# A longer planned distance, from batch 1 on, between attention's TensorE work and what it reads

## The chip, the cores and the metric

One core of a Trainium2 chip. The metric is the device time of one execution in microseconds (us); a kernel's time is the median of its runs. PE is TensorE, PEld its weight loads, DVE VectorE, ACT ScalarE, POOL GpSimd, SP SyncE.

## The reference, cut to what matters

```python
# 8 batches, 12 heads, 448 rows, head size 64
q_n, k_n = q / (norm(q) + 1e-6), k / (norm(k) + 1e-6)
scores = q_n @ k_n.T / tau
attn = softmax(scores)                    # rows
x = heads_side_by_side(attn @ v)          # 8 x 448 x 768
u = x + (x.T @ U @ V).T                   # mixing of rows, U 448x32, V 32x448
out = u + relu(u @ w_ch1) @ w_ch2         # MLP, 768 -> 3072 -> 768
```

## The kernel before

The program first collects operations with their dependencies, durations and buffers, then a list scheduler plans a time for each, and each engine's instructions are emitted in the order of these times. The chip knows only the order and the semaphores. PE takes the first ready operation from a list of streams; the MLP is the last stream and fills what attention leaves.

```python
class Plan:
    SEM = 0.10
    SAFE = 0.25
    LAG = {"PE": 0.16, "ACT": 0.10, "DVE": 0.07, "POOL": 0.0, "SP": 0.0}

    def ready_at(self, op, eng):
        for d in op.deps:
            ...
            else:
                t = max(t, d.end + self.SEM + (self.SAFE if eng == "PE" else 0.0))
        for s in op.acq:          # a buffer of a ring, free again at f
            ...
            t = max(t, f + (self.SEM + self.SAFE if eng == "PE" else self.SEM))

pe_tp, pe_first, pe_av, pe_a, pe_sc, pe_mlp   # PE's streams, first come first

# scores and their exponential, 7 tiles for each pair of heads; three PSUM buffers "sc"
o = Op("PE", pe_t(S), score, deps=qdeps(m), acq=[sc], ...)            # stream pe_sc
Op("ACT", act_t(S), exp, deps=[o], acq=[attn], rel=[sc], ...)

# mixing, first half: U. Four products of 32 output rows each, side by side in one PSUM bank
for t in range(4):
    o = plan.add(Op("PE", pe_t(c1 - c0) + 0.2 if t == 0 else 0.01,
                    lambda ...: nc.tensor.matmul(
        out=mm.tile[R * t:R * (t + 1), 0:c1 - c0], lhsT=U_sb[:, par, t, :],
        rhs=X.tile[:, t, c0:c1], start=True, stop=True),
        deps=need + consts[:2 + par] if t == 0 else (), acq=[mm, A] if t == 0 else []),
        pe_a if c1 < C else pe_av)
```

## Time and profile before

| | before |
|---|---|
| median, first three runs | 607.34 us (607.23 to 607.71) |
| span of the profiled run | 604.8 us |
| PE busy | 586.1 us, 97% |
| DVE, ACT busy | 296.0, 279.5 us |
| PE's first matmul starts at | 7.9 us |
| extra steps of PE from 44 to 435 us, U groups aside | 5.5 us |

PE sets the time. "Step" is the time from the start of one matmul to the start of the next in PE's order; an "extra step" is what a step takes over columns/2.4 + 2.5 ns, summed where it is over some 20 ns (each attention product is 2 ns over, and that is left out). The prediction shows how they are read.

### The profile page before, as it was taken

Reading aid. Unit: us, or ns where it says so; the run is one execution under the profiler, and the core shown is the slowest. Engines: PE = TensorE matmul, PEld = TensorE weight load, DVE = VectorE, ACT = ScalarE, POOL = GpSimd, SP = SyncE. Lnnn points to the kernel's source line nnn. Section 1 sums busy time; section 2 is a strip of 40 time slices with the busy share of each in tenths; the row PEclk is TensorE's granted clock in tenths of the full one; section 3 lists DMA queues with packets and bytes.
Section 4 is the critical chain, followed back from the end, with each engine's and each line's share of the span. In section 5 each row is a group of like instructions: output and inputs, shape, how many; then the busy total and the mean of one; then the engine's idle time right before and its main releaser. Section 6 shows DMA issues by size and latency. Waiting matters only on the chain.

```text
span 604.8 us, 11544 instructions
## 1 busy us (share of the span) xinstructions
PE 586.1 (97%) x4725; PEld 346.8 (57%) x4725; DVE 296.0 (49%) x714; ACT 279.5 (46%) x612; POOL 115.4 (19%) x177
## 2 busy tenths in 40 slices
PE   3899999999999999999999999999999999999997
PEld 1665666555555665666445665666545666654565
DVE  8979679989998987644711253015300210110011
ACT  6977652498782385317641077506442025014300
POOL 8246334071715326000500000000000000000000
PEclk9999999999999999999999999999999999999999
DMA  9999998999999999514902151030002110310021
GB/s 114 202 184 122 208 198 103 173 145 126 129 145 175 151 139 154 83 56 87 154 0 66 46 90 37 1 93 27 15 1 53 52 40 1 92 40 1 0 53 53
DMA packets 150164, 54.58 MB, mean 90 GB/s; under 512 B 115040, under 2 KB 150112, under 8 KB 150112
## 3 DMA queue, kind: packets, MB, share of 16 engines
q0 software_dynamic: 73344, 25.96, 38.6%
q1 hardware_dynamic: 76704, 27.86, 24.2%
q8 instruction: 37, 0.61, 0.4%
q14 instruction: 15, 0.12, 0.1%
q10 hardware_dynamic: 64, 0.02, 0.0%
HBM read 52.25 MB, written 11.01 MB: 105 GB/s over the span
## 4 chain that ended last, share of the span: by engine, by line
PE 92%; ACT 5%; DVE 2%; issue 0%; ACTq 0%
PE mm L785 36%; PE mm L751 35%; PE sc L563 9%; PE av L583 8%; ACT attn L568 3%; PE mm L675 1%; ACT qkT L815 1%; PE tp L365 1%; PE mm L640 1%; DVE ss L452 1%; PE sc L751 1%; DVE xn L527 0%; PE sc L675 0%; ACT uT L815 0%; DVE xn L820 0%
## 5 line engine op out<-in xcount | busy, mean ns | idle before, releaser
L751 PE MATMUL mm<-uT,w_sb 128*128 128x512 bf16 (+1 forms) x1134 | 236.1, 353 | 0.0
L785 PE MATMUL mm<-w_sb,relu 128*128 128x384 bf16 (+1 forms) x1368 | 233.8, 323 | 0.3 <-ACT uT L815 0.3
L568 ACT ACTIVATE attn<-sc 128x448 bf16<-128x448 f32 x336 | 161.0, 565 | 88.8 <-PE av L583 57.4
L785 PEld LDWEIGHTS <-relu 128*128 128x128 bf16 x1368 | 132.6, 98 | 86.7 <-issue 0.9
L751 PEld LDWEIGHTS <-w_sb 128*128 128x128 bf16 x1152 | 111.9, 98 | 101.1 <-issue 1.0
L774 ACT ACTIVATE relu<-mm 128x512 bf16<-128x512 f32 (+1 forms) x169 | 92.4, 547 | 149.2 <-PE mm L751 148.9
L794 DVE TENSOR_TENSOR O_sb<-mm,u_nat 128x384 f32<-128x384 f32 (+1 forms) x57 | 31.0, 547 | 227.1 <-PE mm L785 223.4
L563 PE MATMUL sc<-qkT 128*128 128x448 bf16 x336 | 103.4, 358 | 3.9 <-ACT attn L568 1.9
L583 PEld LDWEIGHTS <-attn 128*128 128x128 bf16 x1536 | 62.7, 98 | 16.0 <-DVE xn L527 0.8
L409 POOL DMA_DIRECT2D v_nat<-in_v_dram x98 | 63.2, 651 | 34.7 <-DMA w_sb<-in_moe_w_ch_dram 13.4
L583 PE MATMUL av<-v_nat,attn 128*128 128x65 bf16 x1536 | 66.6, 194 | 0.2 <-DVE X_sb L592 0.2
L452 DVE TENSOR_REDUCE ss<-sq 112x8 f32<-112x512 bf16 x96 | 63.0, 673 | 0.3
L527 DVE TENSOR_TENSOR xn<-qk_nat,inv 112x512 bf16<-112x512 bf16 (+1 forms) x97 | 62.5, 674 | 0.3
L563 PEld LDWEIGHTS <-qkT 128*128 128x128 bf16 x336 | 29.8, 98 | 24.2 <-issue 8.0
L387 POOL DMA_DIRECT2D qk_nat<-in_q_dram x25 | 17.9, 716 | 130.6 <-DVE xn L527 102.6
L592 DVE TENSOR_TENSOR X_sb<-av,rd 128x256 bf16<-128x256 f32 x96 | 40.0, 419 | 1.5
L590 DVE RECIPROCAL rd<-av 128x4 f32<-128x4 f32 x96 | 17.0, 179 | 38.2 <-PE av L583 36.7
L448 DVE TENSOR_TENSOR sq<-qk_nat 112x512 bf16<-112x512 bf16 x90 | 35.0, 408 | 0.2
L689 DVE TENSOR_TENSOR u_nat<-mm,X_sb 128x384 bf16<-128x384 f32 x36 | 19.1, 553 | 11.0 <-PE mm L675 10.8
L365 PE MATMUL tp<-ident,xn 112*128 112x112 bf16 x144 | 11.7, 226 | 10.0 <-DVE xn L527 9.5
L465 ACT ACTIVATE ln<-ss 112x32 f32<-112x32 f32 (+2 forms) x26 | 6.3, 241 | 32.7 <-DVE ss L452 32.5
L387 POOL DMA_DIRECT2D qk_nat<-in_k_dram x25 | 17.6, 703 | 5.8 <-DMA w_sb<-in_moe_w_ch_dram 5.8
(58 smaller groups left out, 160.8 us busy)
## 6 DMA issues: line engine op xcount, KB each, us to landing
qk_nat<-in_q_dram POOLq DMA_DIRECT2D x23, 224.0 KB, 5.2
qk_nat<-in_k_dram POOLq DMA_DIRECT2D x23, 224.0 KB, 6.4
w_sb<-in_moe_w_ch_dram POOLq DMA_DIRECT2D x4, 1152.0 KB, 14.3
w_sb<-in_moe_w_ch_dram POOLq DMA_DIRECT2D x8, 576.0 KB, 16.6
out_dram<-O_sb SPq DMA_DIRECT2D x15, 168.0 KB, 2.3
out_dram<-O_sb SPq DMA_DIRECT2D x16, 144.0 KB, 2.1
out_dram<-O_sb SPq DMA_DIRECT2D x16, 120.0 KB, 2.0
out_dram<-O_sb SPq DMA_DIRECT2D x16, 96.0 KB, 2.2
```

The source lines that it names most:

```text
L387: ops = [load(lambda i=i, src=src: nc.gpsimd.dma_start(out=ld.tile[:, i, lo:lo + h1 - h0, :], in_=src[b, h0:h1].rearrange("h (s c) d -> s ...
L409: nc.gpsimd.dma_start(out=vb[p0:p0 + s1 - s0, hs, j, 0:D], in_=v[b, hs].rearrange("h (s c) d -> c s h d", c=SC)[c, s0:s1]),
L448: nc.vector.tensor_mul(y, x, x)
L452: lambda i=i, a0=a0, a1=a1, sq=sq: nc.vector.reduce_sum(ss.tile[:, i, a0:a1, :].rearrange("p h c -> p (h c)"), sq.tile[:, 0:a1 - a0, :].re ...
L527: nc.vector.tensor_mul(dst, src, sc)
L563: nc.tensor.matmul(out=sc.tile[:, 0:S], lhsT=kT[:, 128 * m:128 * (m + 1)], rhs=qkT.tile[:, 8:12, :].rearrange("p c s -> p (c s)"), start=T ...
L568: exps[m] = plan.add(Op("ACT", act_t(S), lambda sc=sc, m=m: nc.scalar.activation(out=attn.tile[:, m, off:off + S], in_=sc.tile[:, 0:S], fu ...
L583: nc.tensor.matmul(out=av.tile[:, t, 0:D + 1], lhsT=attn.tile[:, m, 128 * t:128 * (t + 1)], rhs=v_t[b % 2][:, h, j, 0:D + 1], start=(j == ...
L592: muls.append(plan.add(Op("DVE", dve_t(256), lambda av=av, rd=rd, h=h: nc.vector.tensor_mul(X.tile[:, :, h * D:(h + 1) * D], av.tile[:, :, ...
L751: o = plan.add(Op("PE", pe_t(n), lambda cc=cc: nc.tensor.matmul(out=mm.tile[:, 0:n], lhsT=w1_sb[:, cc, f * 128:(f + 1) * 128], rhs=uT.tile ...
L774: nc.scalar.activation(out=relu.tile[:, f, 0:n], in_=mm.tile[:, 0:n], func=AF.Relu)
L785: nc.tensor.matmul(out=mm.tile[:, 0:c1 - c0], lhsT=relu.tile[:, f, i * 128:(i + 1) * 128], rhs=w2_t[:, f, c0:c1], start=(f == 0), stop=(f ...
```

## The change

The intent: attention's instructions shall not stand in PE's queue before their inputs are there, since the MLP's matmuls behind them would stand too. So the 0.25 us that PE's operations keep in the plan from the end of what they wait for becomes 0.8 for the attention of batches 1 to 7.

```diff
-    SAFE = 0.25
+    safe = 0.25
...
     def add(self, op, stream=None):
-        op.seq = self.n
+        op.seq, op.safe = self.n, self.safe
...
-                t = max(t, d.end + self.SEM + (self.SAFE if eng == "PE" else 0.0))
+                t = max(t, d.end + self.SEM + (op.safe if eng == "PE" else 0.0))
...
-            t = max(t, f + (self.SEM + self.SAFE if eng == "PE" else self.SEM))
+            t = max(t, f + (self.SEM + op.safe if eng == "PE" else self.SEM))
...
     state[0] = att(0)
     after = last_mul[-1:]
+    plan.safe = 0.8
     ...                            # attention of batches 1 to 7
+    plan.safe = 0.25
     for b in range(B):
         mlp(b, *state[b])
```

More of the change, by code (lines that the diff above doesn't have):

```diff
@@ L41 @@
 class Op:
-    __slots__ = ("eng", "dur", "fn", "deps", "acq", "rel", "prio", "lat", "start", "end", "by", "seq", "fast")
+    __slots__ = ("eng", "dur", "fn", "deps", "acq", "rel", "prio", "lat", "start", "end", "by", "seq", "fast", "safe")
     def __init__(self, eng, dur, fn, deps=(), acq=(), rel=(), prio=0, lat=0.0, fast=False):
```

## The prediction

> **What bounds the kernel now.** I read the page's busy shares and slices first, then the chain that ended last, then the stretches by stage, and last the waits and the order of PE's instructions around them.
>
> ```profile
> PE 586.1 (97%) x4725; PEld 346.8 (57%) x4725; DVE 296.0 (49%) x714; ACT 279.5 (46%) x612; POOL 115.4 (19%) x177
> ...
> PE   3899999999999999999999999999999999999997
> ...
> PE 92%; ACT 5%; DVE 2%; issue 0%; ACTq 0%
> ```
>
> PE is busy 97% of the span and carries 92% of the chain; only the first slice and the last are visibly thin. So the bound is the number of PE instructions times their step, and all that any order of PE's work can win is the rest. The stretches say where that rest lies:
>
> ```profile
> 0.00:44.00 44.00, 31.62 (x368) 20.27 (x369) 37.92 (x105) 33.47 (x88) 23.62 (x40) 1.00 1.23 165
> 44.00:114.00 70.00, 68.14 (x634) 43.38 (x633) 57.63 (x137) 35.82 (x80) 27.20 (x40) 1.00 1.16 161
> 114.00:240.00 126.00, 125.48 (x1173) 74.36 (x1172) 112.55 (x273) 85.90 (x199) 52.82 (x80) 1.00 1.24 146
> 240.00:435.00 195.00, 194.78 (x1597) 115.68 (x1596) 72.41 (x173) 86.24 (x179) 11.80 (x18) 1.00 0.35 60
> ```
>
> (Columns: stretch, length, busy PE, weight loads, DVE, ACT, POOL, granted clock, DMA share, GB/s.) Idle PE is 12.4 us before 44 us, which is the load of batch 0 and its attention and isn't touched by the change; 1.9 us between 44 and 114 us (batch 1's attention under batch 0's MLP); 0.5 us between 114 and 240; 0.2 us from 240 to 435, where attention ends. After 435 only the MLP runs. Thus idle time alone leaves 2.6 us to win.
>
> Busy time hides more, as a matmul's recorded duration overlaps the next one. I therefore measured from start to start in PE's order. Undisturbed steps are the same all over the trace: 0.162 us for 384 columns, 0.216 for 512, 0.189 for a score tile of 448, 0.032 for an attention product of 65. All steps at their medians sum to 569.1 us; the first matmul starts at 7.9 us, 4.0 us follow the last one's start, and 23.8 us are extra steps, most of them before 44 us. The lines below, from PE's timeline in several stretches, show extra steps between 44 and 435 us:
>
> ```profile
> 58.06 0.33 PE L751 MATMUL mm<-uT,w_sb 128*128 128x384 bf16 x1
> 58.96 0.54 PE L563 MATMUL sc<-qkT 128*128 128x448 bf16 x2 [0.58 <-ACT relu L774]
> ...
> 97.75 0.81 PE L785 MATMUL mm<-w_sb,relu 128*128 128x384 bf16 x4
> ...
> 98.88 1.89 PE L365 MATMUL tp<-ident,u_nat 128*128 128x128 bf16 x24 [0.32 <-DVE O_sb L794]
> ...
> 101.05 0.81 PE L785 MATMUL mm<-w_sb,relu 128*128 128x384 bf16 x4 [0.28 <-ACT uT L815]
> ...
> 147.09 1.10 PE L563 MATMUL sc<-qkT 128*128 128x448 bf16 x3
> 148.03 0.32 PE L675 MATMUL mm<-A_sb,V_sb 128*128 128x384 bf16 x1
> ...
> 181.22 1.42 PE L563 MATMUL sc<-qkT 128*128 128x448 bf16 x4
> 182.49 0.81 PE L785 MATMUL mm<-w_sb,relu 128*128 128x384 bf16 x4
> ...
> 288.95 1.28 PE L563 MATMUL sc<-qkT 128*128 128x448 bf16 x3
> 290.07 0.49 PE L675 MATMUL mm<-A_sb,V_sb 128*128 128x384 bf16 x2
> ```
>
> The reader is to see that one step of 0.162 took 0.90 us at 58 us (the scores wait for their transposed q and k to be copied), and that three score steps took 0.94 us at 147 where 0.57 were due, without any idle time being noted: three score buffers, and the fourth score waits for ACT's exponential on the first.
>
> **What the Trainium skill says.** "TensorE: Matmul & The Clock Gate", section "Back-to-back issue gap", gives N/2.4 + 2.5 ns for the warm gap: 162.5, 215.8, 189.2 ns for 384, 512 and 448 columns. The trace agrees to a nanosecond (the same section's sustained 131 ns for 512 columns doesn't occur here: 216), so PE's steps have nothing left in them and the granted clock is 1.00 everywhere. "Perfetto Trace Analysis", "Tensor Engine Instruction (MATMUL, LD_WEIGHTS)", says that a matmul's end is estimated and only its start recorded; that is why I count steps rather than busy time. The first page, "Part 3: Packing small matmuls", "The mechanism", calls matmuls "strict FIFO, no reordering"; so a score placed too early holds up MLP matmuls behind it that are ready. The trace agrees: at 58.96 us the MLP matmuls queued behind the scores stood too, though the MLP's own lines show 0.3 us of waiting in the whole span.
>
> **The change part by part.** No instruction is added or removed: the same matmuls, the same shapes, the same buffers. A list scheduler in the program decides the order of each engine's instructions by planned times. An instruction of PE counted as ready 0.10 + 0.25 us after the planned end of what it reads, or of what frees its buffer. Now PE's attention work of batches 1 to 7 (294 scores, 1344 attention products, batch 1's transposes, the token mixing in U and V) counts as ready at 0.10 + 0.80; batch 0's attention and the whole MLP stay at 0.25. In the 0.55 us between, three MLP matmuls of 0.162 us go ahead of it. The order changes on PE, and on the other engines as a consequence.
>
> What it can take away, from the steps between 44 and 435 us (extra over the usual step):
> - scores and transposes of batch 1: 0.63 us at 47, 0.57 in five short ones at 52 to 54, 0.74 at 58, 0.37 at 77: 2.31.
> - the transposes of batch 1's mixed rows: 0.48 ahead of them at 98 and 0.85 in and after them (2.17 us from 98.88 to 101.05, less 24 steps of 0.055): 1.33.
> - scores waiting for a score buffer: 0.37 at 147, 0.51 at 181, 0.42 at 226, 0.55 at 289: 1.85.
>
> Together 5.5 us. The groups of four U products cost 0.09 us ahead and 0.10 more than their usual step nearly every time, with and without a wait; I take that for a cost of the form and no gain. With 0.55 us more distance, each extra step shrinks by up to 0.55: of 0.63 and 0.74 stay 0.27; two of the five short steps belong to MLP work, 0.23; the 0.45 us after the last transpose is an MLP matmul's wait and stays. So 5.5 - 0.95 = about 4.5 us are within reach, first order.
>
> What it costs: the planned cycle of a score buffer is 0.189 + 0.16 (score) + 0.10 + 0.427 + 0.10 (exponential) + 0.10 + 0.25 = 1.33 us, a score every 0.44 with three buffers. It becomes 1.88 us, one every 0.63: a batch's 42 scores need at least 26 us in place of 19. The MLP beside one batch is 46.7 us of PE (three tiles: 288 steps of 0.162) or 62.2 (four: 144 of 0.216 and 192 of 0.162), so there is filler, and steps don't depend on which kind follows which. Longer attention costs time only if the MLP runs dry before the next batch's input is mixed. The tightest place is batch 1: its last transposes end at 100.55 us and 72 MLP matmuls, 11.9 us, still follow before batch 1's MLP starts. Its chain from the last normalised pair at 77 us has about two refills of the score buffers and six further links to PE, 8 times 0.55 = 4.4 us. So 7 us of cover remain and nothing is lost there. Later there is more cover: batch 7's attention ends at 430 us, its MLP starts near 539.
>
> As a new order brings some waits of its own, I take 60% of 4.5 us: 2.7 us off. 607.3 - 2.8 = 604.5 us.
>
> **The rivals.**
> 1. *The waits are only moved.* Planned and real times differ by more than 0.55 us, since DVE in the plan is not DVE on the chip: it is busy 113 of 126 us from 114 to 240 and its queue is in order. Then scores wait as often as before, at other places. For it: the wait at 58 us came through a relu on ACT and a copy on DVE, queue effects that no distance sees. Against it: the waits between 114 and 435 us are nearly all score buffers, a short loop that the plan tells well. Time: 606.5 to 608.
> 2. *Attention gets too slow for the early stage.* Between 114 and 180 us it places 80 scores, at 120 to 150 us one every 0.65, next to the new limit of 0.63. Mixed rows could come late, with DVE's rows for the next batch held back too. For it: transfers of q and k already wait for DVE to free their buffers. Against it: PE finds MLP work at all times there (0.5 us idle in 126). Time: 610 to 618, if batch 1 misses its place at 112 us by some us.
> 3. *Everything in reach is won*, and ACT's relus, no longer behind dense rows of exponentials, free PSUM banks earlier: 601.5 to 602.5. This is the floor, because PE's steps alone stand at 569 us and batch 0's start is untouched.
>
> **Range and chances.** Main path 603.5 to 605.5, centre 604.5. Rival 3 sets the low end, 602.0. Rival 1 and a mild form of rival 2 set the high end, 608.0. Faster by over 2% means below 595.2, over twice the waits that exist in the part touched: 1%. Slower by over 2% means above 619.5, only from rival 2 at its worst: 2%. Within 2%: 97%.
>
> **What would show it right or wrong.** Right: the busy shares stay, the counts of PE's groups stay, idle PE between 44 and 435 us falls from 2.6 to about 1 us, rows of three or four scores in a run (as at 147 and 181 us) become rare, single scores stand between MLP matmuls, and the chain's 3% on ACT's exponentials falls to its early part. Attention's last product comes later than 428 us without moving the end. Wrong: a new idle stretch of PE at 100 to 115 us for the mixed rows, MLP matmuls that wait for relu, or extra steps elsewhere that sum to 5 us again. Also wrong if the span before 44 us changes, since batch 0's order is planned against the same competitors only as far as batch 1's work isn't in its way.

## The result, and the profile after

| | before | changed |
|---|---|---|
| median of 4 runs | 607.53 us | 606.24 us |
| ratio | | 0.9977 (95%: 0.996 to 0.9994) |
| start of batch 0's last mixing product in the trace | 40.02 us | 41.51 us |
| from there to the end | 564.79 us | 563.39 us |

Ratios, here and below, are the mean time of one kernel's runs over that of the other's of the same rounds, so not quite the ratio of the medians. The change won 0.23%, half of what was predicted; 606.24 us lies outside the main path (603.5 to 605.5) and inside the outer range.

The two profiled spans are equal, 604.8 and 604.9, and would show no gain. The difference lies before the change begins: up to batch 0's last mixing product PE's order is the same in both, and yet this product came 1.5 us later in this execution. Over all traces with that same start it comes between 40.0 and 41.5 us, with the same 345 matmuls up to it in the same order in all of them. From there to the end, the changed kernel's trace has 1.40 us less, and its second trace (below) 1.44. This interval is what I use from here on and call the rest.

The busy shares and the chain that ended last, from the changed kernel's page:

```profile
PE 587.5 (97%) x4725; PEld 347.2 (57%) x4725; DVE 301.0 (50%) x722; ACT 278.1 (46%) x604; POOL 115.5 (19%) x177
...
PE 93%; DVE 2%; POOL 1%; ACT 1%; DMA 1%; issue 0%; ACTq 0%; POOLq 0%
```

ACT fell from 5% of the chain to 1%, as the prediction asked, and PE has as many matmuls, 4725, but 1.4 us more of busy time. The stretches:

```profile
44.00:114.00 70.00, 69.17 (x638) 43.79 (x636) 54.39 (x130) 37.77 (x83) 27.79 (x41) 1.00 1.17 161
114.00:240.00 126.00, 125.97 (x1173) 74.67 (x1171) 113.55 (x277) 85.45 (x194) 52.87 (x80) 1.00 1.19 145
240.00:435.00 195.00, 195.00 (x1598) 116.18 (x1597) 78.75 (x185) 84.30 (x175) 11.79 (x18) 1.00 0.39 62
```

Idle PE between 44 and 435 us is 0.86 us (0.83, 0.03, 0.00), as against 2.6: "about 1" was predicted. The score buffers no longer hold PE up. PE's timeline near 293 us, where three scores in a row stand again:

```profile
293.44 0.73 PE L563 MATMUL sc<-qkT 128*128 128x448 bf16 x3
294.00 1.67 PE L751 MATMUL mm<-uT,w_sb 128*128 128x512 bf16 x7
```

Three scores take 0.56 us, exactly what is due, where three took 0.94 at 147 us before. Attention's last product starts at 434.5 us instead of 428.3, with no harm. So these waits went as foretold. The sign that the prediction named for it did not come, though: after 110 us rows of three or four scores fell only from 33 to 25, and single scores became fewer, 112 before and 91 after. Most rows stay, and hardly wait. Two things came in place of the waits. The first is a new wait, in PE's timeline:

```profile
50.80 1.17 PE L721 MATMUL mm<-A_sb,V_sb 128*128 128x384 bf16 x3
51.81 0.73 PE L563 MATMUL sc<-qkT 128*128 128x448 bf16 x3
...
53.22 0.79 PE L721 MATMUL mm<-A_sb,V_sb 128*128 128x384 bf16 x2 [0.29 <-DVE u_nat L725]
53.85 0.54 PE L563 MATMUL sc<-qkT 128*128 128x448 bf16 x2
```

L721 are the products that give batch 0's rows by tokens. They belong to the MLP stream, with the short distance; as batch 1's attention now leaves more room ahead of itself, they come (so I read the two traces) while DVE is still reducing batch 1's squares, and wait for DVE's additions to free PSUM banks. Three took 1.01 us in place of 0.49. The second is no wait at all. PE's timeline of a U group before, then of the same group (batch 2, first half) after:

```profile
129.78 0.38 PE L751 MATMUL mm<-uT,w_sb 128*128 128x512 bf16 x1
130.09 0.35 PE L640 MATMUL mm<-X_sb,U_sb 128*32 128x384 bf16 x4
130.37 0.36 PE L563 MATMUL sc<-qkT 128*128 128x448 bf16 x1
```

```profile
135.74 0.34 PE L640 MATMUL mm<-X_sb,U_sb 128*32 128x384 bf16 x1
136.01 0.68 PE L583 MATMUL av<-v_nat,attn 128*128 128x65 bf16 x16
136.62 0.34 PE L640 MATMUL mm<-X_sb,U_sb 128*32 128x384 bf16 x3
136.90 0.55 PE L563 MATMUL sc<-qkT 128*128 128x448 bf16 x2
```

Before, four U products together take 0.28 us. After, sixteen attention products stand between the first and the other three, and one product alone takes 0.27 us and three take 0.28. The four run side by side in the array: the starts within a group are 3 ns apart. So each part of a split group pays the whole pass, and also the step to and from the 128x32 form: 0.09 us ahead (129.78 to 130.09 is 0.31 for a 512-column step of 0.216) and 0.11 behind. From batch 1 on the kernel before has 15 groups, none split. The changed one has 4 split: two of 384 columns (0.269 + 0.275 + 2 x 0.093 against 0.279 + 0.093, so 0.36 us each), one of 512 (0.41) and one of 128 (0.25), 1.37 us together.

The account of the rest, from the steps in both traces:

| | before | changed | difference |
|---|---|---|---|
| extra steps, U groups aside | 5.83 | 3.16 | -2.67 |
| U groups with the step ahead of them (a wait of 0.21 taken out before) | 5.41 | 6.80 | +1.39 |
| after the last matmul's start | 4.00 | 3.79 | -0.21 |
| sum | | | -1.49 (the rest fell by 1.40) |

The 5.83 are the prediction's 5.5 (5.42 read to the ns; of its 0.37 at 77 us 0.11 is the U group's own step) and one of 0.41 at 40 us that is in every kernel.

### The profile page after: what moved, and what is told of

It is laid out like the page before. It is cut to its first block, busy times and chain, and to the rows that moved or that the text cites. A ratio compares the mean times of both kernels' runs of the same rounds, so it can differ in the third digit from the quotient of the medians.

```text
span 604.9 us, 11531 instructions
## 1 busy us (share of the span) xinstructions
PE 587.5 (97%) x4725; PEld 347.2 (57%) x4725; DVE 301.0 (50%) x722; ACT 278.1 (46%) x604; POOL 115.5 (19%) x177
## 4 chain that ended last, share of the span: by engine, by line
PE 93%; DVE 2%; POOL 1%; ACT 1%; DMA 1%; issue 0%; ACTq 0%; POOLq 0%
PE mm L785 36%; PE mm L751 35%; PE sc L563 10%; PE av L583 8%; PE mm L675 1%; PE tp L365 1%; DMA v_nat<-in_v_dram 1%; ACT attn L568 1%; PE mm L640 1%; POOL v_nat L420 1%; POOL qk_nat L387 1%; DVE ss L452 1%; DVE xn L527 1%; PE sc L751 0%; PE sc L675 0%
## 5 line engine op out<-in xcount | busy, mean ns | idle before, releaser
L751 PE MATMUL mm<-uT,w_sb 128*128 128x512 bf16 (+1 forms) x1134 | 239.3, 353 | 0.2 <-DVE u_nat L725 0.2
L785 PE MATMUL mm<-w_sb,relu 128*128 128x384 bf16 (+1 forms) x1368 | 232.0, 323 | 0.0
L568 ACT ACTIVATE attn<-sc 128x448 bf16<-128x448 f32 x336 | 164.1, 554 | 105.5 <-PE av L583 52.6
L785 PEld LDWEIGHTS <-relu 128*128 128x128 bf16 x1368 | 132.8, 98 | 86.2 <-issue 0.2
L751 PEld LDWEIGHTS <-w_sb 128*128 128x128 bf16 x1152 | 112.0, 98 | 103.3 <-issue 1.6
L774 ACT ACTIVATE relu<-mm 128x512 bf16<-128x512 f32 (+1 forms) x158 | 86.7, 549 | 129.7 <-PE mm L751 129.0
L563 PE MATMUL sc<-qkT 128*128 128x448 bf16 x336 | 102.0, 360 | 1.8 <-ACT attn L568 1.5
L563 PEld LDWEIGHTS <-qkT 128*128 128x128 bf16 x336 | 28.5, 98 | 21.0 <-issue 7.0
L776 DVE TENSOR_SCALAR relu<-mm 128x384 bf16<-128x384 f32 (+1 forms) x31 | 18.7, 604 | 12.7 <-PE mm L751 11.9
```

The lines of the kernel that those rows point to most:

```text
L563: nc.tensor.matmul(out=sc.tile[:, 0:S], lhsT=kT[:, 128 * m:128 * (m + 1)], rhs=qkT.tile[:, 8:12, :].rearrange("p c s -> p (c s)"), start=T ...
L568: exps[m] = plan.add(Op("ACT", act_t(S), lambda sc=sc, m=m: nc.scalar.activation(out=attn.tile[:, m, off:off + S], in_=sc.tile[:, 0:S], fu ...
L751: o = plan.add(Op("PE", pe_t(n), lambda cc=cc: nc.tensor.matmul(out=mm.tile[:, 0:n], lhsT=w1_sb[:, cc, f * 128:(f + 1) * 128], rhs=uT.tile ...
L774: nc.scalar.activation(out=relu.tile[:, f, 0:n], in_=mm.tile[:, 0:n], func=AF.Relu)
L785: nc.tensor.matmul(out=mm.tile[:, 0:c1 - c0], lhsT=relu.tile[:, f, i * 128:(i + 1) * 128], rhs=w2_t[:, f, c0:c1], start=(f == 0), stop=(f ...
```

## The experiments

Twelve runs: one is the changed kernel again and one repeats another, so ten new kernels. The theories: A, batch 0's token products took back what batch 1 won. B, batch 1 carries the gain. C, planned times are inexact, and any new order has a few us of waits somewhere. D, the split groups took 1.4 us of a gain that was sized right.

**The change again (again).** No edit.

> The changed kernel once more, for the size and for a second trace. If the size of the first result holds: ratio to before 0.9965 to 0.999 (0.6 to 2.1 us off). If the late start of the first trace (attention of batch 0 was 1.5 us later there, with the same order of instructions) belongs to that execution alone, the last product of batch 0's mixing starts near 40.0 us here and the span is about 1.4 us shorter than the first trace's 604.9; if the change itself causes it, it starts near 41.5 again.

606.00 us against 607.15, ratio 0.9977 (0.9964 to 0.9991). The last mixing product of batch 0 came at 40.9 us, between the two forecasts, and the rest was 563.35. The size holds and the rest repeats; the start wanders from one execution to the next.

**Batch 1 alone (only_b1), batches 2 to 7 alone (from_b2).**

```diff
 only_b1:  for b in range(1, B):
+    plan.safe = 0.8 if b == 1 else 0.25
     state[b] = att(b)
+    plan.safe = 0.25
 from_b2:  for b in range(1, B):
+    plan.safe = 0.25 if b == 1 else 0.8
     state[b] = att(b)
```

> The longer distance for batch 1's attention alone. Theory A (batch 1's waits went, but the products of batch 0's last tokens, which stay at the short distance, took their place and gave 1.6 us back): little is left, 606.5 to 607.5, and the trace shows the waits of those products near 52 us. Theory B (batch 1 carries the gain, as 3.6 of the predicted 5.5 us lay there): 605.5 to 606.3.

> The longer distance from batch 2 on, batch 1 at the short one. Theory A: the score buffers' waits of 1.85 us go and nothing comes in their place, 605.3 to 606.0, as good as the whole change or better. Theory B: 606.5 to 607.3.

only_b1: 606.62 us, 0.9987 (0.9974 to 0.9999), rest 564.06. from_b2: 605.89 us, 0.9977 (0.9964 to 0.9989), rest 563.55. By their medians both fall into A's ranges, though the intervals reach into B's, and only_b1 shows the token products' waits again (1.2 us of extra steps on them). But both also have split groups, three and two, at 0.25 to 0.41 us each; so A wasn't shown by this.

**The token products at the longer distance too (tokens_too).**

```diff
+                plan.safe = 0.8
                 by_tokens(us, *state["first"])
+                plan.safe = 0.25
```

> The change, and the products of batch 0's last tokens at the longer distance as well. Theory A: their 1.6 us of waits shrink to under 0.5 and the kernel gains about 1 us on the changed one, 604.8 to 605.5. Rival C (the planned times are simply not exact, and any new order has some 3 us of waits somewhere): those waits go but others come, 605.7 to 606.7.

605.28 us, 0.9970 (0.9957 to 0.9982). By the median that is A's gain, but the rest says otherwise: 563.02, only 0.33 less than the changed kernel's second trace, and this order has two split groups fewer, worth 0.7. The token products' own waits fell (0.78 us of extra steps left, from 1.23), while 0.84 came back in batch 1's row transposes and 0.49 at an MLP matmul. A's lever moved waits and removed none: the same 0.84 and 0.49 stand in joined_tokens, below.

**The four split groups joined (joined).** The changed kernel's order, with the later products of each split group moved up behind its first; nothing else moves.

```diff
+    for first in [o for o in order if o.seq in u_rest]:   # U groups of batch 1 on
+        rest = u_rest[first.seq]
+        order = [x for x in order if not any(x is y for y in rest)]
+        n = order.index(first) + 1
+        order[n:n] = rest
```

> The changed kernel with its four split groups of U products put together again and nothing else moved. Theory D (the waits fell by the 2.7 us that were predicted, and 1.4 us of that went into four split groups: 0.36 us each for two of 384 columns, about 0.4 and 0.25 for the other two): 1.3 us faster than the changed kernel, ratio to before 0.9950 to 0.9960, and 562.0 us from batch 0's last mixing product to the end where the changed kernel has 563.4. Rival C (a new order simply has new waits): the time after a split group only turns into the next wait, 0 to 0.4 us faster.

603.78 us against 606.98, ratio 0.9952 (0.994 to 0.9965); the rest 561.90, 1.45 us under the changed kernel's 563.35. The ratio and the rest are D's numbers. The changed kernel was not timed in these rounds, so its third, 1.3 us, is read from the rest alone. The extra steps elsewhere did not move (3.11 us in joined2, 3.16 in the changed kernel), so nothing of the gain turned into a new wait. PE's timeline of the same group, from the second run of this order (joined2, below):

```profile
134.00 0.35 PE L641 MATMUL mm<-X_sb,U_sb 128*32 128x384 bf16 x4
134.27 0.68 PE L584 MATMUL av<-v_nat,attn 128*128 128x65 bf16 x16
134.79 0.73 PE L564 MATMUL sc<-qkT 128*128 128x448 bf16 x3
```

0.27 us for the four, and the sixteen products follow once.

**The kernel before with twelve groups split (split_all).** Distance 0.25 everywhere; in each 384-column group the three later products move behind the next PE instruction.

```diff
+    for o in firsts:                        # first products, batch 2 on
+        rest = u_rest[o.seq]
+        order = [x for x in order if not any(x is y for y in rest)]
+        n = order.index(o) + 1
+        while order[n].by != "PE":
+            n += 1
+        order[n + 1:n + 1] = rest
```

> The kernel before with one PE instruction moved into each of its twelve 384-column groups of U products, behind the first product; 24 rows of the order differ. Theory D: 12 x 0.36 = 4.3 us slower, ratio 1.006 to 1.008, each part of a group costing about 0.27 us plus 0.09 ahead of it. Rival: a group's cost is that of its columns and is only divided between the parts, or is hidden by other work: ratio 0.999 to 1.001.

611.47 us against 606.98, ratio 1.0074 (1.0062 to 1.0087), rest 569.33, that is 4.54 more than before for twelve splits, 0.38 each. The cost is real where no wait is involved and nothing else changed. PE's timeline of the group shown above:

```profile
130.09 0.34 PE L641 MATMUL mm<-X_sb,U_sb 128*32 128x384 bf16 x1
130.36 0.36 PE L564 MATMUL sc<-qkT 128*128 128x448 bf16 x1
130.65 0.34 PE L641 MATMUL mm<-X_sb,U_sb 128*32 128x384 bf16 x3
130.93 0.68 PE L584 MATMUL av<-v_nat,attn 128*128 128x65 bf16 x16
```

A score of 0.189 us takes 0.29 between the two parts: 0.10 for the step into the 128x32 form. Both parts take the time of a full pass.

The page "TensorEngine Tiling (Array Packing)" of the Trainium skill, under "Tiling Modes", "Key Properties", names the rule: "Mode switching requires drain: Changing tiling mode (not just tile) drains the TensorE". The steps of 0.09 ahead and 0.11 behind each group fit it, and split_all shows that they are paid for each switch. That the drain is what fills them is the page's word; the runs show the time only.

**Distance 0.5 (d05).** `plan.safe = 0.5`; no group from batch 1 on is split in this order.

> A distance of 0.5 in place of 0.8; no group of U products from batch 1 on is split in this order. Theory D: of 5.5 us of waits some 2.1 stay by the prediction's way of counting, 3.4 go, 2 come new, nothing goes to splits: 1.4 us off, ratio 0.997 to 0.9985, as good as the change. If only the distance counts (rival): half the gain of 0.8 or less, ratio 0.9985 to 1.0.

606.77 us against 606.98, ratio 0.9993 (0.9979 to 1.0006), rest 564.74: nothing won that can be told from zero. D's range is missed; the rival's, 0.9985 to 1.0, holds it. The three largest waits in its trace from 41 to 440 us:

```profile
PE av L583 <- DVE X_sb L592: 0.8, 1, 0.8
PE sc L563 <- ACT attn L568: 0.7, 2, 0.5
PE mm L785 <- DVE O_sb L794: 0.7, 1, 0.7
```

Two of the three wait for DVE's additions and multiplications, which stand in DVE's own queue. This is C: at 0.5 as much comes new as goes, so D's count of the new waits was wrong here; its cost of a split was not at stake. It also says that the 2.7 us at 0.8 are no smooth function of the distance.

**Whole groups and token products (whole1_tokens).** Each U group of batch 1 on is planned as one operation that issues four matmuls, and the token products are at 0.8.

```diff
+            def four(...):
+                for t in range(4):
+                    nc.tensor.matmul(...)
+            o = plan.add(Op("PE", pe_t(c1 - c0) + 0.23, four, deps=..., acq=[mm, A]), ...)
```

> The changed kernel with each group of U products planned as one piece from batch 1 on, and the products of batch 0's last tokens at the longer distance too. Theory D with A: 1.3 us for the splits and 0.5 for the tokens below the changed kernel, ratio to before 0.994 to 0.9955 (603.5 to 604.5 us). Rival C: not below 0.9965.

604.90 us, 0.9964 (0.9952 to 0.9977), rest 562.33. The ratio lies between D with A (0.994 to 0.9955) and C (not below 0.9965), and its interval reaches into both. The rest says more: the splits' share came, the tokens' did not.

**Joined once more, with the tokens, and at 1.2 and 2.0 (joined2, joined_tokens, joined_d12, joined_d20).** The edits are those above; 0.8 is replaced in the last two.

> The changed kernel with its four split groups joined, once more, as the measure for the three beside it. Ratio to before 0.994 to 0.9965, 561.9 us from batch 0's last mixing product to the end.

> Joined, and batch 0's token products at the longer distance too. By the parts (theory A alone): 0.5 us less than joined. Since the run of both with whole groups came out at 562.3 us from batch 0's last mixing product to the end against joined's 561.9, with new waits at batch 1's row transposes, rival C expects no gain: 562.0 to 562.6 there, ratio to before 0.995 to 0.997.

> Distance 1.2 with the groups joined. If more distance only removes more waits: below joined, 561.0 to 561.7 us from batch 0's last mixing product to the end. Rival C (each order has its own waits, whatever the distance): 562.0 to 564.0.

> Distance 2.0 with the groups joined. If more distance only removes more waits: 560.5 to 561.5 us from batch 0's last mixing product to the end. If attention gets too slow for the early stage (the prediction's second rival): an idle stretch of PE before batch 1's MLP and 563 to 567. Rival C: 562 to 564.

| distance, groups joined | median | ratio to before | rest |
|---|---|---|---|
| 0.8 (joined2) | 604.32 us | 0.9944 (0.9932 to 0.9957) | 561.93 |
| 0.8, tokens too | 604.43 us | 0.9952 (0.9938 to 0.9965) | 562.36 |
| 1.2 | 617.09 us | 1.0154 (1.014 to 1.0168) | 574.34 |
| 2.0 | 628.48 us | 1.0341 (1.0327 to 1.0355) | 586.41 |

The kernel before was 607.74 in these rounds. Joined repeats, and is the best version; it beats both kernels. The tokens' longer distance gains nothing on top, which settles A as a lever. At 1.2 and 2.0 (four runs each) every expected range was missed by over 10 us: the prediction's second rival is there, and far worse than I expected of 2.0 (563 to 567). The stretches of joined_d20:

```profile
105.00:110.00 5.00, 4.93 (x45) 3.03 (x43) 4.71 (x11) 3.15 (x9) 0.31 (x1) 1.00 1.36 198
115.00:120.00 5.00, 2.49 (x15) 1.43 (x16) 4.92 (x12) 0.00 (x0) 0.05 (x1) 0.50 0.66 133
125.00:130.00 5.00, 1.34 (x7) 0.24 (x6) 5.00 (x13) 1.79 (x6) 2.14 (x4) 0.73 2.18 140
130.00:135.00 5.00, 1.64 (x7) 0.70 (x7) 4.92 (x13) 1.61 (x6) 4.63 (x7) 0.50 1.46 118
```

and what PE waits for there, from its timeline:

```profile
114.97 1.09 PE L680 MATMUL sc<-A_sb,V_sb 128*128 128x512 bf16 x3 [3.15 <-DVE u_nat L691]
127.49 0.30 PE L641 MATMUL sc<-X_sb,U_sb 128*32 128x128 bf16 x4 [1.85 <-DVE X_sb L593]
133.26 0.29 PE L680 MATMUL sc<-A_sb,V_sb 128*128 128x128 bf16 x1 [1.79 <-DVE u_nat L691]
```

Batch 0's MLP is used up at 109 us (109.5 at 1.2) and batch 1's starts at 138.9 (127.7 at 1.2; 112.1 at 0.8). Between them PE has only attention and mixing, waits for DVE, and its granted clock (the column after POOL) drops to 0.50, which slows what it does have. The Trainium skill tells of this in "TensorE: Matmul & The Clock Gate", "What's actually happening": in its idle state the clock gate passes half of the clock. The trace agrees in the half: the clock falls to 0.50 at 113.7 us, 1.8 us into the idle 3.15 us before 114.97, and a transpose of 128 columns then takes 0.107 us in place of 0.055. PE need not stand still for it: the clock stays there to 123.9 us, though PE is at work in 2.49 of the 5 us from 115 to 120. Why the row mixing falls back so abruptly between 0.8 and 1.2 was not taken apart: DVE is full there (4.9 of 5.0 us at 2.0), and which of its queue's order and the score buffers binds was not separated.

## Why the prediction was right or wrong

- **The bound and the start.** Right: PE's steps carry the time, and nothing before 44 us is the change's doing; the 1.5 us there is an execution's scatter.
- **What can be taken away, 5.5 us, 4.5 in reach.** Right: the waits of scores and transposes, 4.4 us of it, fell to 0.6 (0.47 near 60 us, 0.09 at 191). One reading was wrong: of the five short steps at 52 to 54 us four, not two, end at products of the MLP stream (0.47 us), three of them token products.
- **60% of it as waits come new, 2.7 us net.** The share was a guess, so that the number held is in part luck: extra steps outside the U groups fell by 2.67 us; 4.4 us of the listed ones went (the MLP's 0.45 behind the transposes too, which was to stay) and 1.7 came new. The largest new one, at the token products and the MLP matmul behind them (0.47 us before, 1.63 after), was not foreseen. d05 shows that such a share is no law: at 0.5 nothing was left.
- **What failed: "steps don't depend on which kind follows which", and the U groups' cost as "a cost of the form and no gain".** I saw 0.09 ahead and 0.10 behind each group, took their number, 15, for unchanged ("the counts of PE's groups stay"), and so left a term out of the sum: what a new order does to groups that must stay together. Four were split, 0.25 to 0.41 us each, +1.4 us. 2.7 + 0.2 (the tail) - 1.4 = 1.5 us, and 1.3 was measured (1.4 in the rest). Taking the splits out alone gave 0.9952 and 0.9944; the 604.5 us predicted are the 603.8 and 604.3 us of joined. Twelve splits put into the kernel before cost 4.5 us. The diff and the plan's code had shown that the four products are separate operations and that attention's stream comes first; the skill's page on tiling, which I hadn't looked up, states that a switch of form drains PE.
- **Rival 1 (waits only moved)** took place at 0.5, and with the token products. At 0.8 only half did (3.16 of 5.83 us of extra steps stand).
- **Rival 2 (attention too slow early)** was placed right, before batch 1's MLP. At 0.8 the cover held: batch 1's last row transpose came at 105.6 us in joined2 against 100.5 before, 5.1 us later where 4.4 were counted. At 1.2 the same count would give 7.6 us and leave cover; the run lost 12 us of rest against joined. The count in links is of use near the present order only.
- **Rival 3 (all in reach won)** did not happen; joined's best runs, 603.7 us, are still 1.2 us above its range.
- **Small slips that change nothing.** 88 scores, not 80, start between 114 and 180 us (79 from 120 on). The MLP's own lines wait 0.5 us in the whole span, not 0.3 (0.3 at L785, 0.2 at L751). 2.7 us were taken off as 2.8.

## What to carry to other kernels

When only an order changes, list the instructions whose cost depends on their neighbours (groups that share one pass of the array, forms that PE has to switch between) and count them in the new order as well as the waits: the waits fell here by what was predicted, and half of it was spent on four groups torn apart. Plan such a group as one operation, or put it together again afterwards; with the tokens both ways gave the same rest (562.33 in whole1_tokens, 562.36 in joined_tokens). And a planned distance has an edge: 0.5 gave nothing, 0.8 the best, 1.2 lost 1.5%.

## What the Trainium skill lacked or had wrong

- "TensorEngine Tiling (Array Packing)", "Key Properties", states that a change of tiling mode drains PE but gives no time: here 0.09 us ahead of and 0.11 us behind each group of 128x32 products, so 0.20 us for a round trip, and 0.36 to 0.38 us for a 384-column group torn in two (split_all, after).
- "TensorE: Matmul & The Clock Gate", "Back-to-back issue gap", gives some 131 ns as the sustained spacing of 512-column matmuls and calls columns/2.4 + 2.5 the isolated one. Here the sustained spacing is 216 ns in long unbroken rows, as that formula has it, with a weight load for each.
